# Gated linear attention and a cosine router: rows scattered by expert beside the attention, other block sizes for the experts, and column tiles on TensorE

## The chip, the cores and the metric

The kernel runs on one core of one Trainium2 chip. The metric is the time of one execution on the device in microseconds (us), as the median of several executions; lower is better. A profile of one execution gives its span, from the first to the last instruction.

The engines are TensorE (PE in the rows; PEld is its weight load, a row of its own), VectorE (DVE), ScalarE (ACT), GpSimd (POOL) and SyncE (SP), which issues most of the DMAs. An fp32 matmul stands in the trace as two records, each with a weight load of its own; a transpose on TensorE is one record. "Record" below means this.

## The reference

The first half is a gated linear recurrence with a state of 48 by 48 for each of 4 x 8 heads over 768 tokens. The second half sends each of the 3072 rows of its result (384 columns) to the one of 8 experts whose embedding it resembles most, and runs that expert's two layers on it.

```python
# q, k, v, alpha: (4, 8, 768, 48)
for t in range(S):
    state = alpha[:, :, t, :, None] * state + einsum('bhd,bhe->bhde', k[:, :, t], v[:, :, t])
    y[:, :, t] = einsum('bhd,bhde->bhe', q[:, :, t], state)
x = y.transpose(0, 2, 1, 3).reshape(3072, 384)
logits = normed(x) @ normed(expert_emb).T / tau          # 8 experts
expert_idx = argmax(logits, axis=1)
gate_w = softmax(logits)[arange(N), expert_idx]
for e in range(8):                                       # w1: 384 x 1024, w2: 1024 x 384
    mask = expert_idx == e
    out[mask] = gate_w[mask, None] * (maximum(x[mask] @ w1[e], 0) @ w2[e])
```

Everything is fp32. With the inputs of the reference the experts 0 to 7 get 418, 365, 379, 426, 395, 371, 351 and 367 rows; of the first 16 x 128 tokens expert 0 gets 282.

## The kernel before

**Attention.** The tokens are cut into 24 chunks ("slots") of 128, six for each sequence. A chunk is handled for all eight heads at a time; two heads of 48 columns, padded to 64, fill the 128 partitions, so there are four pairs. A loop over steps `s` (its last lines, after `prepare_experts`) runs four stages of four different chunks in a step: `decays(s)`, `scores(s-1)` and `update(s-1)`, `rows(s-2)`, `logits(s-3)`. `load` fetches alpha, q, k and v two chunks ahead, in pieces of 192 bytes.

- `decays` turns alpha, k and q with TensorE (`turned`, L174: `pa`, `pk`, `pq`, four transposes each). VectorE scans the products of alpha forwards (`a`, L201) and backwards (`r`, L202), each pair of heads by itself: eight scans of 128 columns a chunk. It then makes `kr` (L214) and `qs` (L218).
- `scores` (L267) multiplies `kr` and `qs` head by head: eight matmuls that use 64 of the 128 rows of the array, two of them in different halves. VectorE masks the result (`sm`, L271).
- `update` turns `kr` back (`pkb`, L238), ScalarE copies it (`kb`, L240), four matmuls multiply it with v (`pd`, L243), and the new state is the sum with `decayed` (L231, POOL), on VectorE (L254).
- `rows` makes a chunk of x: four matmuls with the decayed state (L283) and eight with `sm` (L292), all with weights of 128 columns; the rows are copied (L300) and written to DRAM as `x_rows`, in the order of the tokens.
- `logits` turns x (L309) and multiplies it with the embeddings (`pl`, L316). After six chunks `choose` finds the expert and the gate of their tokens.

**Routing**, after the last chunk. `rk` (L348, L351) ranks each token among those of its expert, VectorE makes of it a place in blocks of 128 rows, each expert's last block being filled up, and 24 matmuls (`inv`, L398) invert the sort: which token stands in which row of which block.

**Experts.** There are 31 blocks, as many as 3072 rows can need at most. For each block POOL gathers 128 rows of `x_rows` (`xg`, L459), TensorE turns them (`pxg`, L469), 24 matmuls of 128 moving columns make the first layer (`ph`, L478), ScalarE takes the positive part (L484), eight matmuls of 384 columns make the second layer (`pyo`, L488), VectorE multiplies with the gate (L492), and POOL scatters the rows to the output (L493). SP loads the two weight tensors of a block's expert (L451, L454), where they aren't in the buffer yet.

Nothing in this kernel fixes the order of instructions beyond the order of the code: a scheduler arranges each engine's queue.

Of the kernel before, what the change touches and what calls it, by code (L numbers as in the profile page):

```python
# [15 lines left out]
SP = mybir.EngineType.SP  # L16

# [6 lines left out]
def kernel(  # L24
# [25 lines left out]
    NBLK = (N + E * (P - 1)) // P  # L50
    FAR = 1 << 20  # a row index out of bounds: the row is skipped

    x_rows = nc.dram_tensor("x_rows", (N, DM), FP32, kind="Internal").ap()
# [7 lines left out]
    make_upper_triangular(nc, causal[:, 0], val=1.0, diag=True)  # L61
    earlier = consts.tile([P, P], FP32)  # [j, i] = 1 where j < i
    make_upper_triangular(nc, earlier, val=1.0, diag=False)
    ones = consts.tile([P, P], FP32)
    nc.gpsimd.memset(ones, 1.0)
    zeros = consts.tile([P, P], FP32)
    nc.gpsimd.memset(zeros, 0.0)
    half = consts.tile([P, NP, 2], FP32)  # which head of the pair a partition is of
    nc.gpsimd.memset(half, 0.0)
    nc.gpsimd.memset(half[0:DP, :, 0:1], 1.0)  # L70
    nc.gpsimd.memset(half[DP:P, :, 1:2], 1.0)
    cols_i = consts.tile([P, P], I32)
    nc.gpsimd.iota(cols_i, pattern=[[1, P]], base=0, channel_multiplier=0)
    cols = consts.tile([P, P], FP32)
    nc.vector.tensor_copy(cols, cols_i)
    toks_i = consts.tile([P, NS], I32)
    nc.gpsimd.iota(toks_i, pattern=[[P, NS]], base=1, channel_multiplier=1)
    toks = consts.tile([P, NS], FP32)  # token + 1
    nc.vector.tensor_copy(toks, toks_i)
    first = consts.tile([P, E], FP32)  # E, E-1, ..: the first of equal logits wins  # L80
    nc.vector.tensor_scalar(first, cols[:, 0:E], -1.0, float(E), ALU.mult, ALU.add)

# [1 line left out]
    lg = consts.tile([P, NS, E], FP32)  # L84
    sq = consts.tile([P, NS], FP32)
    gate = consts.tile([P, NS], FP32)
    chosen = consts.tile([P, NS, E], FP32)
    before = consts.tile([P, NS + 1, E], FP32)
    nc.gpsimd.memset(before[:, 0], 0.0)
    rtau = consts.tile([P, 1], FP32)  # L90
    embT = consts.tile([P, KT, E], FP32)
    gidx = consts.tile([P, NBLK], I32)
    sidx = consts.tile([P, NBLK], I32)
    bgate = consts.tile([P, NBLK], FP32)
    eblk = consts.tile([1, NBLK], I32)
    fresh = consts.tile([1, NBLK], I32)

    # ==== gated linear attention, a chunk of P tokens of all heads at a time ====
    with ExitStack() as c1:
        pads = c1.enter_context(tc.tile_pool(name="pads", bufs=1))  # L100
        loads = c1.enter_context(tc.tile_pool(name="loads", bufs=6))
# [3 lines left out]
        ps_mm = c1.enter_context(tc.tile_pool(name="ps_mm", bufs=3, space=PSUM))  # L105

        NBUF = 4
        at_s = [pads.tile([P, H, DP], FP32, name=f"at{i}") for i in range(NBUF)]
        qt_s = [pads.tile([P, H, DP], FP32, name=f"qt{i}") for i in range(NBUF)]
        kt_s = [pads.tile([P, H, DP], FP32, name=f"kt{i}") for i in range(NBUF)]  # L110
        for i in range(NBUF):
            nc.gpsimd.memset(at_s[i][:, :, D:DP], 1.0)
            nc.vector.memset(qt_s[i][:, :, D:DP], 0.0)
            nc.vector.memset(kt_s[i][:, :, D:DP], 0.0)
        NR = 3
        r_s = [pads.tile([P, NP, P], FP32, name=f"r{i}") for i in range(NR)]
        for i in range(NR):
            nc.vector.memset(r_s[i][:, :, P - 1 : P], 1.0)
# [4 lines left out]
        def prepare_experts():  # L123
            emb = work.tile([E, DM], FP32, name="emb", bufs=1)
            nc.scalar.dma_start(out=emb, in_=expert_emb)
            nc.scalar.dma_start(out=rtau, in_=tau.to_broadcast([P, 1]))
            nc.vector.reciprocal(rtau, rtau)
# [405 lines left out]
```

## Time and profile before

| what | us |
|---|---|
| median of 3 runs (the runs: 627.73, 634.01, 628.14) | 628.14 |
| span of the profiled execution | 625.4 |
| TensorE busy in it | 554.2 |
| VectorE busy | 201.9 |
| ScalarE busy | 100.9 |
| GpSimd busy | 93.7 |

The span is the only time that the profile gives of its own execution; the median of the runs lies 2.7 us above it, and what stands around the first and the last instruction is taken to be that. "Busy" is the time in which at least one instruction of the engine ran; matmuls are pipelined, so the time that a group of them takes is read from the start of its first record to the start of the first record of the next group, not from the durations. [...]

### The profile page before, as it was taken

Reading aid. Unit: us, or ns where it says so; the run is one execution under the profiler, and the core shown is the slowest. Engines: PE = TensorE matmul, PEld = TensorE weight load, DVE = VectorE, ACT = ScalarE, POOL = GpSimd, SP = SyncE. Lnnn points to the kernel's source line nnn. Section 1 sums busy time; section 2 is a strip of 40 time slices with the busy share of each in tenths; the row PEclk is TensorE's granted clock in tenths of the full one; section 3 lists DMA queues with packets and bytes.
Section 4 is the critical chain, followed back from the end, with each engine's and each line's share of the span. In section 5 each row is a group of like instructions: output and inputs, shape, how many; then the busy total and the mean of one; then the engine's idle time right before and its main releaser. Section 6 shows DMA issues by size and latency. Waiting matters only on the chain.

```text
span 625.4 us, 9640 instructions
## 1 busy us (share of the span) xinstructions
PE 554.2 (89%) x3804; PEld 463.9 (74%) x3804; DVE 201.9 (32%) x608; ACT 100.9 (16%) x202; POOL 93.7 (15%) x149
## 2 busy tenths in 40 slices
PE   5799989889989965389999999999999999999994
PEld 4688878788878855268778787787877877878773
DVE  6967676757765527101010010100101001010010
ACT  2222422422241240001101011011110100101100
POOL 1110110010011101311011120220211112011010
PEclk9999999988995985579999999999999999999998
DMA  9979886636710000760757658166175775811000
GB/s 152 173 128 150 126 123 124 129 67 124 129 39 14 26 25 2 260 243 26 249 181 244 236 192 275 38 239 219 51 248 195 233 258 166 298 39 38 0 1 0
DMA packets 130508, 85.37 MB, mean 137 GB/s; under 512 B 102199, under 2 KB 121699, under 8 KB 130464
## 3 DMA queue, kind: packets, MB, share of 16 engines
q1 hardware_dynamic: 126336, 73.93, 46.4%
q0 software_dynamic: 3968, 10.82, 4.9%
q8 instruction: 30, 0.49, 0.3%
q14 instruction: 14, 0.11, 0.1%
q10 hardware_dynamic: 160, 0.01, 0.0%
HBM read 122.50 MB, written 10.81 MB: 213 GB/s over the span
## 4 chain that ended last, share of the span: by engine, by line
PE 72%; DVE 13%; issue 8%; ACT 2%; DMA 2%; POOL 1%; POOLq 0%; ACTq 0%
PE ph L478 24%; PE pyo L488 22%; PE py L292 7%; PE py L283 4%; DVE a L201 4%; PE pd L243 3%; DVE r L202 3%; PE pl L316 3%; DMA xg<-x_rows,gidx 2%; PE pa L174 2%; PE inv L398 2%; PE sc L267 2%; DVE kr L214 1%; PE px L309 1%; DVE xgT L471 1%
## 5 line engine op out<-in xcount | busy, mean ns | idle before, releaser
L478 PEld LDWEIGHTS ph<-xgT,w 128*128 128x128 f32 x1488 | 172.1, 194 | 14.3 <-DVE xgT L471 9.8
L478 PE MATMUL ph<-xgT,w 128*128 128x128 f32 x1488 | 174.6, 278 | 6.8 <-DVE xgT L471 6.8
L488 PE MATMUL pyo<-w,hT 128*128 128x384 f32 x496 | 165.1, 486 | 0.0
L488 PEld LDWEIGHTS pyo<-w,hT 128*128 128x128 f32 x496 | 91.9, 190 | 57.5
L492 DVE TENSOR_SCALAR y<-pyo,bgate 128x384 f32<-128x384 f32 x31 | 19.2, 618 | 303.1 <-PE pyo L488 303.1
L484 ACT ACTIVATE hT<-ph 128x512 f32<-128x512 f32 x62 | 37.0, 597 | 345.2 <-PE ph L478 345.2
L493 POOL DMA_INDIRECT out_dram<-y,sidx x31 | 31.1, 1003 | 178.8 <-DVE y L492 175.2
L292 PE MATMUL py<-vt,sm 128*128 128x48 f32 x384 | 56.4, 277 | 0.0
L292 PEld LDWEIGHTS py<-vt,sm 128*128 128x128 f32 x384 | 53.0, 203 | 0.0
L459 POOL DMA_INDIRECT xg<-x_rows,gidx x31 | 32.2, 1037 | 135.4 <-PE pxg L469 115.0
L201 DVE TENSOR_TENSOR_SCAN a<-pa,zeros 128x128 f32<-128x128 f32 x96 | 38.9, 405 | 22.0 <-PE pa L174 22.0
L202 DVE TENSOR_TENSOR_SCAN r<-pa,zeros 128x127 f32<-128x127 f32 x96 | 38.1, 397 | 0.0
L283 PE MATMUL py<-decayed,qs 128*128 128x96 f32 x160 | 35.6, 306 | 0.0
L271 DVE TENSOR_TENSOR sm<-sc,causal 128x512 f32<-128x512 f32 x48 | 31.1, 679 | 1.9 <-PE sc L267 1.9
L267 PE MATMUL sc<-qs,kr 64*128 64x128 f32 x384 | 30.6, 302 | 0.0
L267 PEld LDWEIGHTS sc<-qs,kr 64*128 64x128 f32 x384 | 25.6, 203 | 4.7 <-issue 3.8
L243 PE MATMUL pd<-vt,kb 128*128 128x96 f32 x160 | 23.3, 290 | 4.7 <-ACT kb L240 4.7
L231 POOL TENSOR_TENSOR decayed<-state,ends 128x384 f32<-128x384 f32 x20 | 16.6, 830 | 71.1 <-DVE state L254 56.9
L238 PE MATMUL pkb<-ident,kr 128*128 128x128 f32 x80 | 13.4, 291 | 15.5 <-DVE r L202 15.5
L469 PE MATMUL pxg<-ident,xg 128*128 128x128 f32 x93 | 15.0, 298 | 13.7 <-issue 8.5
L218 DVE SCALAR_TENSOR_TENSOR qs<-pq,rend,a 128x128 f32<-128x128 f32 x96 | 27.0, 341 | 0.0
L243 PEld LDWEIGHTS pd<-vt,kb 128*128 128x128 f32 x160 | 20.0, 196 | 8.9 <-ACT kb L240 8.9
(115 smaller groups left out, 382.4 us busy)
## 6 DMA issues: line engine op xcount, KB each, us to landing
w<-in_moe_w_dram SPq DMA_DIRECT2D x62, 1536.0 KB
at<-in_alpha_dram SPq DMA_DIRECT2D x24, 192.0 KB
qt<-in_q_dram SPq DMA_DIRECT2D x24, 192.0 KB
kt<-in_k_dram SPq DMA_DIRECT2D x24, 192.0 KB
vt<-in_v_dram SPq DMA_DIRECT2D x24, 192.0 KB
x_rows<-x SPq DMA_DIRECT2D x24, 192.0 KB
xg<-x_rows,gidx POOLq DMA_INDIRECT x31, 5.4
out_dram<-y,sidx POOLq DMA_INDIRECT x31, 3.0
```

What stands on the lines that cost most here:

```text
L201: nc.vector.tensor_tensor_scan(a[:, p], pa[:, p], zeros, 1.0, ALU.mult, ALU.add)
L202: nc.vector.tensor_tensor_scan(r[:, p, P - 2 :: -1], pa[:, p, P - 1 : 0 : -1], zeros[:, 0 : P - 1], 1.0, ALU.mult, ALU.add,)
L243: nc.tensor.matmul(pd[:, 2 * p * D : 2 * (p + 1) * D], lhsT=kb[:, p], rhs=vt[:, 2 * p : 2 * p + 2].rearrange("p h d -> p (h d)"), start=Tr ...
L267: nc.tensor.matmul(sc[:, hh, p], lhsT=kr[sl, p], rhs=qs[sl, p], start=True, stop=True)
L271: nc.vector.tensor_tensor(sm[:, hh], sc[:, hh], causal.to_broadcast([P, NP, P]), ALU.mult)
L283: nc.tensor.matmul(py[:, 2 * p * D : 2 * (p + 1) * D], lhsT=qs[:, p], rhs=decayed[:, p].rearrange("p j e -> p (j e)"), start=not opened, s ...
L292: nc.tensor.matmul(py[:, h * D : (h + 1) * D], lhsT=sm[:, hh, p], rhs=vt[:, h], start=not opened, stop=True, skip_group_check=True,)
L459: nc.gpsimd.indirect_dma_start(out=xg, out_offset=None, in_=x_rows, in_offset=bass.IndirectOffsetOnAxis(ap=gidx[:, j : j + 1], axis=0), bo ...
L478: nc.tensor.matmul(ph[:, f], lhsT=w1_t[:, i, (f0 + f) * P : (f0 + f + 1) * P], rhs=xgT[:, i], start=(i == 0), stop=(i == KT - 1),)
L484: nc.scalar.activation(hT[:, f0 : f0 + 4], ph, AF.Relu)
L488: nc.tensor.matmul(py, lhsT=hT[:, f], rhs=w2_t[:, f], start=(f == 0), stop=(f == FT - 1))
L493: ins = nc.gpsimd.indirect_dma_start(out=out, out_offset=bass.IndirectOffsetOnAxis(ap=sidx[:, j : j + 1], axis=0), in_=y, in_offset=None, ...
```

## The change

It rewrites most of the kernel; the mathematics stays.

- **Rows scattered beside the attention.** The chunks are put into ten groups of one to three (`GROUPS`). After a group's rows are there, `choose` and `place` find each token's expert and rank, and POOL scatters the rows, with logits and token number (393 columns), to `xs`, where each expert has a region of 3072 rows (`to_rows`). The routing at the end, the gather and the inversion of the sort go.
- **Two early blocks.** After 16 chunks the first expert with 256 rows leads (`first_expert`). Its first 256 rows are fetched and its weights loaded during the attention; the first layer of these two blocks runs in the last three steps (`first_layer_early`), where chunks run out.
- **Three static blocks an expert.** Each expert then gets 384 rows in one go, the leading one 128: the first layer has 384 moving columns. Where an expert has more rows, a branch that TensorE, ScalarE, VectorE, POOL and SP each take by a value in memory runs a half block of 64 rows (`run_extra`); anything beyond that is in `run_rest`, behind another branch. By the counts above the experts 0, 3 and 4 need one half block each, and `run_rest` isn't entered. The rows of a block lie one behind the other in `xs` and are fetched by plain DMAs (`fetch`); `pads` fills up the last block with blank rows. Gates are worked out from the fetched rows (`gates`).
- **Scans over all pairs.** Row 0 of alpha and a second operand restart the product at each pair's border, so a chunk needs one scan of 511 and one of 512 columns. `qs` moves to POOL, the copy of `pq` and half of the mask to ScalarE and POOL.
- **Column tiles, and y in two banks.** `update`, `mix_states`, `mix_chunk`, `rows` and `half_block` write their results to 64 of the 128 partitions, each matmul with weights of 64 columns; neighbours write to different halves, and y is kept transposed in two PSUM banks (`pyx`). `rows` turns it back and makes the logits in the same matmuls (`sel`).
- **TensorE in written order**: `in_turn` issues each group behind the last TensorE instruction before it.

The core of the diff:

```diff
+    GROUPS = (
+        (0, 3), (3, 6), (6, 9), (9, 12), (12, 14), (14, 16), (16, 19), (19, 21), (21, 23), (23, 24)
+    )
+    S0, EARLY = 16, 2
...
+        def to_rows(rows, x):
+            ins = nc.gpsimd.indirect_dma_start(
+                out=xs,
+                out_offset=bass.IndirectOffsetOnAxis(ap=rows, axis=0),
+                in_=x,
...
-            for p in range(NP):
-                nc.vector.tensor_tensor_scan(a[:, p], pa[:, p], zeros, 1.0, ALU.mult, ALU.add)
-                nc.vector.tensor_tensor_scan(
-                    r[:, p, P - 2 :: -1], pa[:, p, P - 1 : 0 : -1], zeros[:, 0 : P - 1],
-                    1.0, ALU.mult, ALU.add,
-                )
+            nc.vector.tensor_tensor_scan(
+                r[:, L - 2 :: -1], pa[:, L - 1 : 0 : -1], inr[:, L - 2 :: -1],
+                1.0, ALU.mult, ALU.add,
+            )
...
+            by_pool = nc.gpsimd.tensor_tensor(
+                qs.rearrange("p n t -> p (n t)"), d["qc"], a, ALU.mult
+            )
...
+        def update(s):
...
+                    mm(
+                        pd[DP * hh : DP * hh + DP, p],
+                        lhsT=kb[:, h * DP : (h + 1) * DP],
+                        rhs=vt[:, h],
+                        start=True, stop=True,
+                    )
...
+        def mix_states(s):
...
+                            mm(
+                                pyx[hh][to : to + DP, q * P : (q + 1) * P],
+                                lhsT=dec[sl, p], rhs=d["qs"][sl, p],
+                                start=(q == 0), stop=False, skip_group_check=True,
+                            )
...
+        def mix_chunk(s):
...
+                    mm(
+                        pyx[hh][to : to + DP, q * P : (q + 1) * P],
+                        lhsT=vt[:, 2 * p + hh], rhs=sm[hh][:, p],
+                        start=("dec" not in d and q == 0), stop=True, skip_group_check=True,
+                    )
...
+        def rows(s):
...
+                        mm(
+                            px[sl, hh, q], lhsT=yT[hh][:, q, sl], rhs=sel[:, hh, q],
+                            start=True, stop=True, skip_group_check=True,
+                        )
...
+        def first_layer(w1_t, hT, xT, f, n):
+
+            ph = ps_h.tile([P, 512], FP32, name="ph")[:, 0:n]
+            for i in range(KT):
+                nc.tensor.matmul(
+                    ph, lhsT=w1_t[:, i, f * P : (f + 1) * P], rhs=xT[:, i],
+                    start=(i == 0), stop=(i == KT - 1),
+                )
...
+        def half_block(w1_t, w2_t, xT, gate, col):
...
+                        for i in range(2):
+                            c0 = (f0 + f) * P + i * HALF
+                            nc.tensor.matmul(
+                                ph[i * HALF : (i + 1) * HALF, f * HALF : (f + 1) * HALF],
+                                lhsT=w1_t[:, k, c0 : c0 + HALF], rhs=xT[:, k],
+                                start=(k == 0), stop=(k == KT - 1), skip_group_check=True,
+                            )
...
+        def run_extra(i):
...
+            with tc.If(more > 0):
+                half_block(
...
-        for j in range(NBLK):
...
+        for i in range(E):
+            if i + 2 < E:
+                weights(i + 2)
+                to_rows(pads[:, i + 2 : i + 3], blank)
+                fetch(i + 2)
+            run(i)
+            run_extra(i)
+            if i == 3:
+                run_rest(i % NW)
```

How the instructions stand now. TensorE, one chunk in the middle of the attention, before (L174 turns, L267 scores, L238 turns `kr` back, L309 turns x, L243 is the state, L283 and L292 are the rows):

```order
L174 MATMUL pa<-ident,at_123 128x128 x4
L174 MATMUL pk<-ident,kt_131 128x128 x4
L174 MATMUL pq<-ident,qt_127 128x128 x4
L267 MATMUL sc<-qs,kr 128x128 x8
L238 MATMUL pkb<-ident,kr 128x128 x4
L309 MATMUL px<-ident,x 128x128 x3
L243 MATMUL pd<-vt,kb 128x96 x4
L283 MATMUL py<-decayed,qs 128x96
L292 MATMUL py<-vt,sm 128x48 x2
```

The last two rows come three times more, and then `pl` (three matmuls). The same engine and place now (line numbers are those of the changed kernel, where all matmuls of the attention are recorded at L187 and all transposes at L190; `dec` is the decayed state, `ycols` the transposed y):

```order
L187 MATMUL pyx_478<-qs,dec 64x128
L187 MATMUL pyx_479<-qs,dec 64x128
L187 MATMUL pyx_478<-sm_370,vt_128 64x128 x4
L187 MATMUL pyx_479<-sm_371,vt_128 64x128 x4
L187 MATMUL pd<-vt_129,kb 64x64 x8
L187 MATMUL px<-sel,ycols_488 64x104 x4
L187 MATMUL px<-sel,ycols_489 64x104 x4
L190 MATMUL pkb<-ident,kr 128x128 x4
L190 MATMUL pa<-ident,at_115 128x128 x4
L190 MATMUL pk<-ident,kt_123 128x128 x4
L190 MATMUL pq<-ident,qt_119 128x128 x4
```

The first two rows stand there four times in turn, and eight matmuls of the scores follow behind `pq`. The rows of a chunk and its state have become 32 matmuls with results on 64 partitions, and the turn of x and the logits are one group, `px`.

TensorE, from the last chunk to the first expert, before:

```order
L309 MATMUL px<-ident,x 128x128 x3
L316 MATMUL pl<-embT,xT 128x8 x3
L348 MATMUL rk<-before,ones 128x200
L351 MATMUL rk<-chosen,earlier 128x192
L398 MATMUL inv<-put,in_row 128x62 x24
L469 MATMUL pxg<-ident,xg 128x128 x15
L478 MATMUL ph<-xgT,w_0_2664 128x128 x24
L488 MATMUL pyo<-w_0_2666,hT 128x384 x8
```

And now (`phe` is the early first layer; the `pyo` rows before L843 are the second layers of the two early blocks):

```order
L187 MATMUL rk<-before,ones 128x16
L187 MATMUL rk<-chosen,earlier 128x16
L187 MATMUL phe<-exT,w_0_93 128x256 x6
L187 MATMUL rk<-before,ones 128x8
L187 MATMUL rk<-chosen,earlier 128x8
L187 MATMUL rk<-before,ones 128x8
L187 MATMUL phe<-exT,w_0_93 128x256 x6
L854 MATMUL pyo<-w_0_95,ehT 128x384 x10
L796 MATMUL pxg<-ident,xg_90 128x128 x3
L796 MATMUL pxg<-ident,xg_90 128x64 x3
L854 MATMUL pyo<-w_0_95,ehT 128x384 x6
L843 MATMUL ph<-xT_2981,w_0_93 128x128 x6
```

Between the last `rk` and the first `pxg`, which needs rows that are still to be scattered and fetched, there now stand 6 + 10 matmuls of the early blocks.

TensorE, in the middle of the experts, before:

```order
L478 MATMUL ph<-xgT,w_0_2664 128x128 x24
L488 MATMUL pyo<-w_0_2666,hT 128x384 x8
L469 MATMUL pxg<-ident,xg 128x128 x6
L478 MATMUL ph<-xgT,w_1_2665 128x128 x24
L488 MATMUL pyo<-w_1_2667,hT 128x384 x8
```

And now, the end of one expert's turn (L873 and L886 are the half block, which L923 jumps over where it isn't needed):

```order
L843 MATMUL ph<-xT_2982,w_1_94 128x384 x6
L796 MATMUL pxg<-ident,xg_92 128x128 x3
L843 MATMUL ph<-xT_2982,w_1_94 128x384 x6
L796 MATMUL pxg<-ident,xg_92 128x64 x3
L854 MATMUL pyo<-w_1_96,hT 128x384 x24
L919 TENSOR_LOAD extra
L923 COMPARE_AND_BRANCH
L873 MATMUL ph<-xT_2982,w_1_94 64x64 x48
L886 MATMUL pyo<-w_1_96,hT_half 64x384 x8
L923 UNCONDITIONAL_BRANCH x2
```

One expert is one run of 24 + 24 matmuls of 384 columns with the next expert's transposes between them.

## Rows read from the trace of the kernel before

**Rows 1.** Busy time and clock by stage: attention, routing, experts (windows).
```profile
core 0: us, PE busy (x) PEld busy (x) DVE busy (x) ACT busy (x) POOL busy (x), PEclk, DMA share, GB/s
15.00:222.00 207.00, 183.94 (x1593) 167.47 (x1592) 141.85 (x437) 54.80 (x124) 23.90 (x57) 0.94 0.59 103
222.00:270.00 48.00, 21.74 (x114) 19.16 (x115) 18.12 (x69) 5.71 (x12) 9.97 (x14) 0.59 0.35 128
270.00:612.00 342.00, 335.25 (x2048) 267.93 (x2047) 31.72 (x58) 36.42 (x61) 55.72 (x55) 0.99 0.48 163
```

**Rows 2.** Timeline of TensorE, one chunk at full clock (start, length, what).
```profile
100.04 1.13 PE L243 MATMUL pd<-vt,kb 128*128 128x96 f32 x8
101.01 0.39 PE L283 MATMUL py<-decayed,qs 128*128 128x96 f32 x2
...
103.65 0.80 PE L316 MATMUL pl<-embT,xT 128*128 128x8 f32 x6
104.30 0.63 PE L174 MATMUL pa<-ident,at 128*128 128x128 f32 x4
104.77 0.60 PE L174 MATMUL pk<-ident,kt 128*128 128x128 f32 x4
105.21 0.60 PE L174 MATMUL pq<-ident,qt 128*128 128x128 f32 x4
105.74 1.16 PE L267 MATMUL sc<-qs,kr 64*128 64x128 f32 x16
106.83 0.46 PE L283 MATMUL py<-decayed,qs 128*128 128x96 f32 x2
```

**Rows 3.** Two stretches of 2 us around a fall of the clock (windows).
```profile
130.00:132.00 2.00, 0.52 (x10) 0.33 (x6) 2.00 (x10) 0.24 (x1) 0.33 (x2) 1.00 0.85 174
136.00:138.00 2.00, 2.00 (x12) 2.00 (x11) 0.00 (x0) 0.00 (x0) 0.66 (x1) 0.50 0.00 0
```

**Rows 4.** Chain that ended last, in order of time (start, length, what).
```profile
34.66 0.85 PE pl L316 x6
...
143.82 1.72 PE sc L267 x16
...
371.41 5.62 PE ph L478 x48
377.03 5.16 PE pyo L488 x16
382.20 5.36 PE ph L478 x48
387.55 5.18 PE pyo L488 x16
```

**Rows 5.** Groups by line and shape (busy us, mean ns of one; idle before).
```profile
L201 DVE TENSOR_TENSOR_SCAN a<-pa,zeros 128x128 f32<-128x128 f32 x96 | 38.9, 405 | 22.0 <-PE pa L174 22.0
L231 POOL TENSOR_TENSOR decayed<-state,ends 128x384 f32<-128x384 f32 x20 | 16.6, 830 | 71.1 <-DVE state L254 56.9 <-ACT state L252 14.2
L214 DVE TENSOR_TENSOR kr<-pk,r 128x512 f32<-128x512 f32 x24 | 16.5, 689 | 0.5
L240 ACT COPY kb<-pkb 128x512 f32<-128x512 f32 x20 | 11.7, 587 | 73.0 <-PE pkb L238 73.0
```

**Rows 6.** Timeline from the last chunk to the first expert, and the end.
```profile
227.53 0.83 PE L316 MATMUL pl<-embT,xT 128*128 128x8 f32 x6 [0.57 <-ACT xT L313]
...
230.94 0.21 DVE L157 TENSOR_TENSOR chosen<-sel,best 128x48 f32<-128x48 f32 x1
...
242.07 10.50 PE L398 MATMUL inv<-put,in_row 128*128 128x62 f32 x48 [7.51 <-POOL put L393]
...
253.99 1.21 POOL L459 DMA_INDIRECT xg<-x_rows,gidx  x1 [11.97 <-DVE sidx L411]
...
270.40 7.63 PE L478 MATMUL ph<-xgT,w 128*128 128x128 f32 x48
...
617.57 0.62 DVE L492 TENSOR_SCALAR y<-pyo,bgate 128x384 f32<-128x384 f32 x1 [9.90 <-PE pyo L488]
618.47 0.98 POOL L493 DMA_INDIRECT out_dram<-y,sidx  x1 [9.54 <-DVE y L492]
```

**Rows 7.** DMA early in the attention (window), and the scatters of the output.
```profile
15.00:20.00 5.00, 4.33 (x44) 3.80 (x44) 4.26 (x12) 1.07 (x2) 0.83 (x1) 1.00 1.36 170
...
DMA to landing us min/median/max: 2.1/3.0/7.9
```

More of the change, by code (lines that the diff above doesn't have):

```diff
@@ L80 @@
+    part = consts.tile([P, 1], FP32)
+    starts_i = consts.tile([P, NC + 1], I32)
+    starts = consts.tile([P, NC + 1], FP32)
+    blank = consts.tile([P, ROW], FP32)
     first = consts.tile([P, E], FP32)
[L81 to L86, printed above, removed]
+    ebase = consts.tile([P, E], FP32)
     chosen = consts.tile([P, NS, E], FP32)
     before = consts.tile([P, NS + 1, E], FP32)
-    nc.gpsimd.memset(before[:, 0], 0.0)
@@ new lines, with weights @@
+    NW = 3
+    w1_s = [consts.tile([P, KT, F], FP32, name=f"w1_{i}") for i in range(NW - 1)]
+    w2_s = [consts.tile([P, FT, DM], FP32, name=f"w2_{i}") for i in range(NW - 1)]
+    w1_r = w1.rearrange("e (k p) f -> e p k f", p=P)
+    w2_r = w2.rearrange("e (k p) d -> e p k d", p=P)
+    def weights(i):
+        e = nc.values_load(
+            turn_i[0:1, i : i + 1], engines=(SP,), min_val=0, max_val=E - 1,
+            skip_runtime_bounds_check_because="a sum of two experts, less E from E on",
+        )
+        nc.sync.dma_start(
+            out=w1_s[i % NW], in_=w1_r[ds(e, 1)].rearrange("e p k f -> (e p) k f")
+        )
+        nc.sync.dma_start(
+            out=w2_s[i % NW], in_=w2_r[ds(e, 1)].rearrange("e p k d -> (e p) k d")
+        )
@@ new lines, in fetch_early, with mm @@
+    def fetch_early():
+        lead = nc.values_load(
+            turn_i[0:1, 0:1], engines=(SP,), min_val=0, max_val=E - 1,
+            skip_runtime_bounds_check_because="a sum of two experts, less E from E on",
+        )
+        ins = nc.sync.dma_start(
+            out=xg_s[NXG - 1][:, 0:EARLY],
+            in_=xs[ds(lead * N, EARLY * P)].rearrange("(t p) r -> p t r", p=P),
+        )
+        tc.add_to_no_dep_group("xs", ins.ins)
+    last = {}
+    def mm(*args, **kwargs):
+        last["pe"] = nc.tensor.matmul(*args, **kwargs)
@@ L258, in scores @@
+            carried["state"] = state = work.tile([P, NP, DP], FP32, name="state")
+            if c == 0:
+                nc.vector.tensor_copy(state, pd)
+            else:
+                nc.vector.tensor_tensor(state, pd, d["dec"], ALU.add)
         def scores(s):
@@ L325, with warm @@
+        def warm(n):
+            pw = ps_mm.tile([P, P], FP32, tag="mm", name="pw")
+            for _ in range(n):
+                mm(pw, lhsT=ident, rhs=ident, start=True, stop=True)
+        send = []
+        warm(7)
+        fixed_parts()
         load(0)
+        a0 = prepare_loads()
+        prepare_fills()
         load(1)
-        prepare_experts()
         for s in range(NS + 3):
-            if s + 2 < NS:
+            if s + 2 <= NS:
                 load(s + 2)
+            if 0 <= s - 1 < NS:
+                with in_turn():
+                    keys_back(s - 1)
@@ new lines, in second_layer @@
+        def second_layer(w2_t, hT, gate, col, last=False):
+            py = ps_y.tile([P, DM], FP32, name="pyo")
+            y = yp.tile([P, DM], FP32, name="y")
+            for f in range(FT):
+                nc.tensor.matmul(
+                    py, lhsT=hT[:, f], rhs=w2_t[:, f], start=(f == 0), stop=(f == FT - 1),
+                )
+            cut = DM // 2 if last else DM
+            nc.vector.tensor_scalar(y[:, 0:cut], py[:, 0:cut], gate, None, ALU.mult)
+            if last:
+                nc.scalar.mul(y[:, cut:], py[:, cut:], gate)
+            scatter(y, col)
```

924 lines of the change are left out of this document (608 added, 316 removed).

## The prediction

> **What bounds the kernel now.** I read the windows by stage first, then the timeline of TensorE within a chunk, the chain that ended last, the groups by shape, and the hand-off from the last chunk to the first expert.
>
> The windows show three stages [rows 1]. In the attention TensorE is busy 183.94 of 207 us, in the experts 335.25 of 342; in the 48 us of routing it is busy for less than half, at 0.59 of its clock. So two stages are worth what they cost TensorE, and the third is a chain of others. The chunks come every (227.53 - 34.66) / 23 = 8.39 us, from the first `pl` to the last [rows 4, 6].
>
> Inside a chunk the price is the record, not the columns it moves [rows 2]. From start to start, `pd` takes 0.97 us for 8 records of 96 columns (0.121), the 24 records of `py` 2.64 us (0.110, though most move 48), `pl` 0.65 for 6 records of 8 columns (0.108), four transposes 0.47 (0.117). Only `sc`, whose neighbours use different halves of the array, is cheaper: 16 records in 1.09 us, 0.068 each. In the experts the first layer takes 5.36 to 5.62 us for 48 records of 128 columns (0.112), the second 5.16 for 16 of 384 (0.323) [rows 4]; there the columns do count, 0.323 for three times 0.112. [...]
>
> In the hand-off, the last `pl` is at 227.53, the last choice at 230.94, the inversion takes 10.50 us from 242.07, the first gather is issued at 253.99, and the first layer starts at 270.40 [rows 6].
>
> **The attention.** A chunk now has on TensorE 16 transposes x 0.117 = 1.87; the scores as before, 1.09; `mix_states`, 16 records; and `mix_chunk`, `pd` and `px` with 16 records each, their results on 64 partitions, their weights 64 columns wide. No row shows such a record. It is bounded by 0.110, where halves don't overlap at all, and by 0.034, half of `sc`'s price, as the weights are half as wide. The nearest row is `sc`, two tiles at a time; I take 0.060, a little under its 0.068, and 0.050 for `mix_states`, which has four places in the array. That is 48 x 0.060 + 0.80 = 3.68. Changing between tile shapes costs about 0.09: from the first `pq` to the first `sc` it is 0.53 us, against 0.44 for `pk` [rows 2]; five changes make 0.4. In all 7.04. The first chunk of a sequence has no `mix_states`, the last no `pkb` and `pd`: (0.80 + 0.47 + 0.96) x 4/24 = 0.37 less. I add 0.2 for waits in the written order: the bank of `pa` comes free only after the second scan, and every third chunk VectorE's choice stands ahead of it. So 6.87 us a chunk instead of 8.39.
>
> The others stay below. VectorE: a scan of 512 columns is at most four of 0.405 [rows 5], 1.62; two of them, `kr` and a mask at 0.69 each, and the state with some ten small operations, for which I allow 1.3, make 5.9 at most, and its eight scans of before were 3.2 of it. ScalarE: three copies of 512 at 0.587 and three smaller, 3.0. POOL: `qs` and `dec` at 0.830 per 384 columns [rows 5], 1.1 + 0.6, a mask of 512 at the same price per column, 1.1, a scatter of 1.0 [rows 6], and fills, 4.4. DMA: 786 KB of loads and 201 KB of scattered rows at the 170 GB/s of 15 to 20 us [rows 7] are 5.8. If TensorE's records came at 0.034, this 5.8 would be the bound, and nothing under it is to be had.
>
> Start: q of chunk 3 lies behind 2.95 MB at 170 GB/s, 17.3 us and a landing of at least 2.1 [rows 7], so step 3 starts at about 20, and step 24 at 20 + 21 x 6.87 = 164.3. The last steps hold 48 records of the early first layer at 256/384 x 0.323 = 0.215 (10.3), one more `sc` (1.1), the rows of two chunks (5.4), `rk` (1.1) and 6 transposes (0.7): to 182.9.
>
> **The hand-off.** Routing, gather and inversion go; late next is the leading expert's remaining rows. After the last `rk`: three VectorE operations (0.9), three scatters and a blank one, 1.0 each behind each other on POOL, a landing of 3.0, 0.4 that I allow for SP's values and issue, another landing of 3.0 [rows 6, 7]: 11.3. TensorE has meanwhile 12 records of 0.215 and 20 of 0.323, 9.0. So 2.3 us of waiting; with landings of 7.9 it would be 12, with 2.1 nearly none. Queued behind the waiting `pxg` are the second early block and all experts, so a wait here is paid in full. Early second layers 32 x 0.323 = 10.3, 6 transposes 0.7, the wait: to 196.2.
>
> **The experts.** Leading expert: 5.4 + 5.2 and 12 transposes, 1.4: to 208.2. Seven times 96 records of 0.323 are 217.1, with 72 transposes 8.4: to 433.7. That is 24 blocks instead of 31; the first layer's own gain, three of 0.112 for one of 0.323, is nothing worth the name. Three half blocks: 96 records at 0.060 (5.8), 0.7 waiting for ScalarE, 16 records at about 0.17 (2.8): 9.3 each, 28, to 461.6. They save little against a whole block of 10.5. No row shows a branch on TensorE; between nothing (it is taken while matmuls are still queued) and a landing of 3.0 each I take 0.4, as the queue ahead is 24 matmuls, eight times: 3.2. Weights, 3.1 MB per 31 us, and the gates stay beside it. The end stays: from the last y at 617.57 to 625.4 [rows 6], 8. Sum 472.8, against the span of 625.4; with the 2.7 that the median lies above the span, **475 us**.
>
> [...]
>
> **Rivals.**
> - *Each change of shape drains.* A record's length is 0.63 - 3 x 0.117 = 0.28 [rows 2]; five make 1.4 instead of 0.4, and 24 chunks 24 us more: 499. Against it: only 0.09 is seen at `sc`.
> - *The halves don't overlap.* 0.110 instead of 0.060: (24 + 24 + 20) x 16 x 0.05 = 54, `mix_states` 20 x 16 x 0.06 = 19, half blocks 3 x 7.2 = 22: 571. For it: every full-height record costs 0.11; against it: `sc`.
> - *The clock stays low in the attention.* At 0.50 `sc` takes 1.72 [rows 4], 1.58 times 1.09; 6.87 x 0.58 x 24 = 95 more: 570. For it: a fall after 2 us of little work [rows 3]; against it: that wait was for VectorE's eight scans and choice, which shrink.
> - *Slower than before*: records on 64 partitions run one behind the other at their full length. There are 68 x 16 + 20 x 16 + 3 x 112 = 1744; at 0.28 each, 0.22 more, the time is 859. It is slower from 153 / 1744 + 0.060 = 0.148 us a record on. Nothing in the trace is pipelined so badly.
> - *Not what it says*: if a half block were entered for all eight experts, five more of 9.3 make 521; the counts of rows say three.
>
> **How the numbers follow.** Forecast 0.67; changes that drain 0.12; no overlap 0.09; low clock 0.07; eight half blocks 0.01; slower 0.03; within 1% (about what a measurement of this kernel tells from no change) 0.01, for a mixture of the dear ones. The cheap end is 5.8 a chunk, 22 less, and half blocks 10 cheaper: 443. The high end takes in the draining changes, all of the hand-off's 10 and branches' 14: 525. Left out are the two cases at 570 and what is slower, 0.2.
>
> **What would show it.** Right: `pxg` of the leading expert near 190 us, chunks 6.9 apart, `mix_chunk`, `pd` and `px` near 0.06 a record, a run of 24 + 24 matmuls in 31 us, clock at 1.00 from chunk 3 on. Wrong: TensorE waiting in the chunks for VectorE or POOL, records near 0.11, the clock at 0.50 for long, or gaps of some us behind each expert's last `pyo`.

## The result and the profile after

The changed kernel takes 453.01 us (median of 4 runs, 451.56 to 453.83), the kernel before beside it 630.39; the ratio is 0.7182 with a 95% interval of 0.7134 to 0.723. The forecast was 475, the range 443 to 525. The profiled execution has a span of 451.3, and TensorE is busy for 431.3 of it.

The stages of the changed kernel (windows; they answer to [rows 1]; columns as there):

```profile
15.00:162.00 147.00, 141.57 (x2161) 122.39 (x2159) 110.41 (x241) 67.82 (x141) 91.97 (x160) 1.00 0.95 190
162.00:168.30 6.30, 6.30 (x36) 5.71 (x35) 3.66 (x30) 1.63 (x4) 2.96 (x3) 1.00 0.18 64
168.30:443.20 274.90, 271.14 (x1195) 162.37 (x1194) 46.27 (x158) 78.44 (x173) 33.27 (x34) 0.99 0.31 107
```

The stage of routing, 48 us at a clock of 0.59 before, is gone, and TensorE's granted clock (PEclk, as a share of its full speed) is 0.99 to 1.00 in all three. Its timeline shows one chunk (answering to [rows 2]), the hand-off ([rows 6]), one half block and the branch behind it:

```profile
94.71 1.16 PE L187 MATMUL sc<-qs,kr 64*128 64x128 f32 x16
95.80 0.67 PE L187 MATMUL pyx<-qs,dec 64*64 64x128 f32 x16
96.40 1.09 PE L187 MATMUL pyx<-sm,vt 128*64 128x128 f32 x16
97.32 0.64 PE L187 MATMUL pd<-vt,kb 128*64 128x64 f32 x16
97.78 0.89 PE L187 MATMUL px<-sel,ycols 128*64 128x104 f32 x16
98.60 0.66 PE L190 MATMUL pkb<-ident,kr 128*128 128x128 f32 x4
99.09 0.60 PE L190 MATMUL pa<-ident,at 128*128 128x128 f32 x4
99.53 0.61 PE L190 MATMUL pk<-ident,kt 128*128 128x128 f32 x4
99.99 0.66 PE L190 MATMUL pq<-ident,qt 128*128 128x128 f32 x4
100.57 1.16 PE L187 MATMUL sc<-qs,kr 64*128 64x128 f32 x16
...
161.09 0.94 PE L187 MATMUL px<-sel,ycols 128*64 128x104 f32 x16
...
165.45 0.37 PE L187 MATMUL rk<-before,ones 128*128 128x8 f32 x2
165.68 2.84 PE L187 MATMUL phe<-exT,w 128*128 128x256 f32 x12
168.35 6.61 PE L854 MATMUL pyo<-w,ehT 128*128 128x384 f32 x20
174.80 0.82 PE L796 MATMUL pxg<-ident,xg 128*128 128x128 f32 x6
...
296.28 3.02 PE L873 MATMUL ph<-xT,w 128*64 128x64 f32 x96
299.13 3.45 PE L886 MATMUL pyo<-w,hT_half 128*64 128x384 f32 x16
305.74 5.83 PE L843 MATMUL ph<-xT,w 128*128 128x384 f32 x12 [3.16 <-ACTq L936]
311.41 0.49 PE L796 MATMUL pxg<-ident,xg 128*128 128x128 f32 x3
```

From `sc` to `sc` a chunk takes 5.86 us instead of 8.39, and TensorE waits for nothing in it. From start to start, a record with narrow weights costs 0.029 us in `pd` (0.46 / 16), 0.051 in `px`, 0.058 in `mix_chunk`, 0.037 in `mix_states`; changes of the tile shape between groups are contained in these prices. The hand-off shows no wait in front of `pxg`. A half block takes 2.85 + 3.38 = 6.2 us. The one gap is in front of the last but one row: 3.16 us at L936, the branch of `run_rest`, and the 12 records behind it take 5.67 us where the same 12 take 3.97 elsewhere.

The scans, per line ([rows 5]): one of 512 columns takes 1.222 us, as long as three of 128 did (0.405 each).

```profile
L498 DVE TENSOR_TENSOR_SCAN a<-pa,ini 128x512 f32<-128x512 f32 x24 | 29.3, 1222 | 0.8
L502 POOL TENSOR_TENSOR qs<-qc,a 128x512 f32<-128x512 f32 x24 | 30.6, 1276 | 34.0 <-DVE a L498 24.1 <-ACT ycols L607 4.3 <-ACT sm L567 3.9
```

Where the 174.1 us between the two spans come from, with the early blocks' work (12.1 us) counted with the experts:

| stage | before | after | less by |
|---|---|---|---|
| attention, to the end of the last `pl` or `px` | 228.2 | 155.2 | 73.0 |
| routing, to the first matmul of an expert | 42.2 | 1.1 | 41.1 |
| experts, to the last y | 347.2 | 287.1 | 60.1 |
| end | 7.8 | 8.0 | -0.2 |

### The profile page after: what moved, and what is told of

Its sections match the earlier page's. It is cut to its first block, busy times and chain, and to the rows that moved or that the text cites. A ratio compares the mean times of both kernels' runs of the same rounds, so it can differ in the third digit from the quotient of the medians.

```text
span 451.3 us, 9164 instructions
## 1 busy us (share of the span) xinstructions
PE 431.3 (96%) x3474; PEld 301.0 (67%) x3474; DVE 172.5 (38%) x464; ACT 154.7 (34%) x330; POOL 138.3 (31%) x230
## 4 chain that ended last, share of the span: by engine, by line
issue 53%; PE 26%; DVE 7%; POOL 5%; DMA 4%; another core or an unknown queue 2%; ACT 1%; POOLq 1%; DVEq 0%; ACTq 0%
PE pyx L187 6%; PE sc L187 4%; POOL out_dram L781 3%; PE px L187 3%; PE pyo L854 2%; PE pa L190 2%; PE pq L190 2%; PE pk L190 2%; PE pkb L190 2%; DVE r L474 2%; PE phe L187 2%; PE pd L187 1%; DMA xs<-x,dest 1%; DMA out_dram<-y,sx 1%
## 5 line engine op out<-in xcount | busy, mean ns | idle before, releaser
L843 PE MATMUL ph<-xT,w 128*128 128x384 f32 (+1 forms) x384 | 120.8, 466 | 3.8 <-ACTq L936 3.2
L854 PE MATMUL pyo<-w,hT 128*128 128x384 f32 x352 | 115.6, 488 | 0.0
L843 PEld LDWEIGHTS ph<-xT,w 128*128 128x128 f32 x384 | 68.4, 192 | 46.9 <-issue 5.7
L854 PEld LDWEIGHTS pyo<-w,hT 128*128 128x128 f32 x352 | 66.3, 190 | 45.3
L847 ACT ACTIVATE hT<-ph 128x384 f32<-128x384 f32 (+1 forms) x64 | 29.7, 465 | 141.4 <-PE ph L843 141.4
L502 POOL TENSOR_TENSOR qs<-qc,a 128x512 f32<-128x512 f32 x24 | 30.6, 1276 | 34.0 <-DVE a L498 24.1
L474 DVE TENSOR_TENSOR_SCAN r<-pa,inr 128x511 f32<-128x511 f32 x24 | 29.2, 1215 | 5.7 <-PE pa L190 5.5
L498 DVE TENSOR_TENSOR_SCAN a<-pa,ini 128x512 f32<-128x512 f32 x24 | 29.3, 1222 | 0.8
L309 POOL DMA_INDIRECT xs<-x,dest x24 | 24.8, 1032 | 11.2 <-DVE best L332 4.0
L187 PE MATMUL sc<-qs,kr 64*128 64x128 f32 x384 | 28.1, 286 | 0.0
L187 PE MATMUL pyx<-sm,vt 128*64 128x128 f32 x384 | 26.5, 279 | 0.2 <-POOL sm L568 0.2
L187 PEld LDWEIGHTS sc<-qs,kr 64*128 64x128 f32 x384 | 23.5, 189 | 4.2 <-issue 3.4
L187 PEld LDWEIGHTS pyx<-sm,vt 128*64 128x64 f32 x384 | 20.4, 136 | 4.4 <-issue 3.3
L187 PE MATMUL px<-sel,ycols 128*64 128x104 f32 x384 | 21.5, 254 | 0.0
L187 PEld LDWEIGHTS px<-sel,ycols 128*64 128x64 f32 x384 | 17.7, 137 | 1.2 <-issue 0.7
```

The costliest lines, as they stand in the source:

```text
L187: last["pe"] = nc.tensor.matmul(*args, **kwargs)
L309: ins = nc.gpsimd.indirect_dma_start(out=xs, out_offset=bass.IndirectOffsetOnAxis(ap=rows, axis=0), in_=x, in_offset=None, bounds_check=E ...
L474: nc.vector.tensor_tensor_scan(r[:, L - 2 :: -1], pa[:, L - 1 : 0 : -1], inr[:, L - 2 :: -1], 1.0, ALU.mult, ALU.add,)
L498: d["a_scan"] = by_dve = nc.vector.tensor_tensor_scan(a, pa, ini, 0.0, ALU.mult, ALU.add)
L502: by_pool = nc.gpsimd.tensor_tensor(qs.rearrange("p n t -> p (n t)"), d["qc"], a, ALU.mult)
L843: nc.tensor.matmul(ph, lhsT=w1_t[:, i, f * P : (f + 1) * P], rhs=xT[:, i], start=(i == 0), stop=(i == KT - 1),)
```

## Experiments

The question was why the chunks and half blocks came out cheaper than forecast, and what else the 475 had wrong. Spans are compared with the 451.3 of the changed kernel, medians with its 453.0.

**Half blocks without column tiles.**

```diff
-                        for i in range(2):
-                            c0 = (f0 + f) * P + i * HALF
...
-                                ph[i * HALF : (i + 1) * HALF, f * HALF : (f + 1) * HALF],
-                                lhsT=w1_t[:, k, c0 : c0 + HALF], rhs=xT[:, k],
...
+                        c0 = (f0 + f) * P
...
+                            ph[:, f * HALF : (f + 1) * HALF],
+                            lhsT=w1_t[:, k, c0 : c0 + P], rhs=xT[:, k],
```

and the second layer's eight matmuls all write to the lower half, `py[0:HALF]`.

> The half blocks without column tiles: the first layer as 48 records of 64 columns with weights of 128 columns, the second as 16 records of 384 columns. Theory (a record with full-height weights costs 0.112 us however few columns it moves): 48 x 0.112 + 16 x 0.323 = 10.5 instead of 6.23, for three half blocks 13 more: 466. Rival (only columns are paid, 0.029 for 64): 1.4 + 5.2 = 6.6, 1 more: 454.

Measured: 466.09 us (466.01 to 466.22). The timeline of its TensorE, with the next expert's first row as the end:

```profile
191.72 5.47 PE L872 MATMUL ph<-xT,w 128*128 128x64 f32 x48
197.11 5.38 PE L884 MATMUL pyo<-w,hT_half 128*64 128x384 f32 x16
202.42 3.81 PE L843 MATMUL ph<-xT,w 128*128 128x384 f32 x11
```

10.7 us a half block, 0.112 a record of 64 columns (5.39 / 48), as much as the records of 128 columns cost before: at full height 64 columns are no cheaper than 128, and column tiles save 13 us here. The second layer's 16 records, which all write to one half, cost 0.332, against 0.323 at full height, so narrow weights alone made nothing cheaper here.

**The same half for neighbours.**

```diff
-            for p in range(NP):
-                for hh in range(2):
+            for hh in range(2):
+                for p in range(NP):
```

and likewise in `rows` and `half_block` (the half outermost); `mix_chunk` takes the pairs as (0, 2, 1, 3).

> The same column-tile matmuls, with neighbours that write to the same half of the partitions (pd, px, mix_chunk, half blocks; mix_states is left as it is). Theory: the low price (pd 0.029 us a record, px 0.051, mix_chunk 0.058, half block 0.030 and 0.211) is that of two halves at work side by side. Then each doubles: pd +0.46, px +0.82, mix_chunk +0.92 a chunk, 2.2 x 24 = 53, and 6.2 more for each of three half blocks, 19: about 525. Rival 1: a record is paid by the columns that it moves, whatever its neighbour: 453, as it is. Rival 2: alone, a record costs the 0.110 of a full-height one: (16 x 0.110 x 3 - 2.2) x 24 = 74 and (96 x 0.110 + 16 x 0.323 - 6.2) x 3 = 29 more: about 555.

Measured: 469.12 us (467.96 to 469.33), between all that was expected.

```profile
100.36 1.14 PE L187 MATMUL pyx<-sm,vt 128*64 128x128 f32 x16
101.28 0.74 PE L187 MATMUL pd<-vt,kb 128*64 128x64 f32 x13
```

`mix_chunk`, now four records to one half and four to the other, still takes 0.92 for its 16; `pd`, eight and eight, 0.75 (101.28 to 102.03); the half block's first layer, 24 and 24, about 5.0 (199.33 to its last three records at 204.27) instead of 2.85. None doubled. That the halves work side by side survives only if records for the other half start ahead of their turn, as a `px` at 101.81 does here, ahead of two `pd` written before it that start at 101.86, and that was tested.

**Long runs in one half.**

```diff
-            for hh in range(2):
-                for p in range(NP):
+            for p in (0, 2, 1, 3):
+                for hh in range(2):
```

in `mix_chunk`, and `rows` with `lhsT=yT[hh][:, q]` of 128 columns.

> Two parts. mix_chunk writes eight records to one half, then eight to the other (in the changed kernel two and two; in the run same_half four and four, which cost nothing, 0.92 us for the 16), and both copies of y come behind them. rows is written with full-height weights of 128 columns: 8 records of 104 columns instead of 16. Theory: each half of the array works off its own records one behind the other at the price of a full-height one, 0.84 ns a column, 0.108 for 128; the halves run side by side as long as TensorE finds a record for the other half among the next three or four. Then the 16 records of mix_chunk take (16 - 3.5) x 0.108 = 1.35 instead of 0.92; in same_half so did pd (0.75 instead of 0.46) and px. The rows cost 8 x 0.108 = 0.86 instead of 0.82, as full-height records of few columns do. With up to 0.5 more a chunk for the later copies, 24 x (0.47 to 0.97): 464 to 476. Rival: a 128-column record costs 0.058 with narrow weights in whatever order: mix_chunk stays at 0.92, and 454 to 466.

Measured: 464.50 us (462.91 to 465.05). Timeline of its TensorE:

```profile
103.20 1.25 PE L187 MATMUL pyx<-sm,vt 128*64 128x128 f32 x13
104.18 0.27 PE L187 MATMUL pd<-vt,kb 128*64 128x64 f32 x1
104.29 0.27 PE L187 MATMUL pyx<-sm,vt 128*64 128x128 f32 x1
104.29 0.22 PE L187 MATMUL pd<-vt,kb 128*64 128x64 f32 x1
104.40 0.27 PE L187 MATMUL pyx<-sm,vt 128*64 128x128 f32 x1
104.40 0.27 PE L187 MATMUL pd<-vt,kb 128*64 128x64 f32 x1
104.51 0.27 PE L187 MATMUL pyx<-sm,vt 128*64 128x128 f32 x1
104.51 0.73 PE L187 MATMUL pd<-vt,kb 128*64 128x64 f32 x13
105.17 1.14 PE L187 MATMUL px<-sel,ycols 128*128 128x104 f32 x8
106.15 0.60 PE L190 MATMUL pkb<-ident,kr 128*128 128x128 f32 x4
```

The last three records of `mix_chunk`, in the upper half, start every 0.11 us, and beside them `pd` already runs in the lower half, though it is written behind them. `mix_chunk` takes 104.51 + 0.11 - 103.20 = 1.42 us, by the theory (16 - 3) x 0.108 = 1.40. So in these runs the price is that of the full array, 0.84 ns a column (0.108 / 128; in the kernel before 5.18 / 16 / 384 [rows 4]), once for each half, and work for the other half starts up to three records ahead of its turn: two and two or four and four, the 16 take 0.92, eight and eight 1.42. `px` at full height takes 0.98 and the `pkb` behind it 0.43, together 0.10 more than the 0.82 + 0.49 with tiles: there tiles bring next to nothing.

**More changes of the tile shape.** `mix_states` and `mix_chunk` mixed, first two and two (120 more changes), then four and four (40 more).

```diff
+            for q in range(NQ):
+                for j in range(2):
+                    for i in range(2):
+                        state_mm(i, 2 * q + (i + j) % 2)
+                    for i in range(2):
+                        chunk_mm(i, 2 * q + (i + j) % 2)
```

> mix_states and mix_chunk are mixed, two matmuls of the one and two of the other in turn, neighbours still in different halves: six more changes of the tile shape in each of the 20 chunks that have a state, 120 in all, and no other work. Theory (the rows of the changed kernel show hardly more than 0.1 us at a change): between 0 and 120 x 0.09 = 11 more, 453 to 464. Rival, that each change drains the engine for the 0.28 us of a record's length: 34 more, 487.

Measured: 482.74 us (482.56 to 483.68), above the theory's 464 and near the rival's 487. Its timeline:

```profile
96.49 0.44 PE L187 MATMUL pyx<-qs,dec 64*64 64x128 f32 x4
96.86 0.44 PE L187 MATMUL pyx<-sm,vt 128*64 128x128 f32 x4
97.23 0.44 PE L187 MATMUL pyx<-qs,dec 64*64 64x128 f32 x4
...
99.06 0.44 PE L187 MATMUL pyx<-sm,vt 128*64 128x128 f32 x4
99.33 0.64 PE L187 MATMUL pd<-vt,kb 128*64 128x64 f32 x16
```

The eight groups take 2.84 us instead of 1.52. Two records on each of two places are 0.216, and a group takes 0.37, so 0.15 is the change; but the states also lost two of their four places here. The second run keeps those, with four groups of eight records:

> mix_states and mix_chunk in turn by q: four matmuls of the states (all four places of the array, as before), four of the chunk (halves in turn), and once more: two more changes of the tile shape in each of 20 chunks, 40 in all, and nothing else. Theory, from the run with 120 more changes (29.7 us more, of which 20 x 0.44 because the states there used two places at a time instead of four): 0.15 to 0.17 a change, 6.4 more, 459.5. Rival 1: all of the 29.7 was changes, 0.25 each: 10 more, 463. Rival 2: all of it was the lost places: 453.

Measured: 458.71 us (456.45 to 459.10), span 457.0: 5.7 for 40 changes, 0.14 each.

```profile
98.09 0.45 PE L187 MATMUL pyx<-qs,dec 64*64 64x128 f32 x8
98.47 0.66 PE L187 MATMUL pyx<-sm,vt 128*64 128x128 f32 x8
99.06 0.45 PE L187 MATMUL pyx<-qs,dec 64*64 64x128 f32 x8
99.44 0.66 PE L187 MATMUL pyx<-sm,vt 128*64 128x128 f32 x8
99.92 0.64 PE L187 MATMUL pd<-vt,kb 128*64 128x64 f32 x16
```

The rows agree: the 32 records take 1.83 us instead of 1.52, 0.155 for each of two changes. That is more than a row of the unchanged order lets see, and half of the rival's 0.28.

**No written order.**

```diff
-        return tc.issue_after(last["pe"].ins) if last else ExitStack()
+        return ExitStack()
```

> TensorE's written order is taken out (in_turn does nothing), the scheduler arranges the matmuls of the attention as it did in the kernel before. Theory: the records' sum, 5.87 us a chunk, stays the bound, and the order only keeps TensorE from waiting; with the share of idle time of the attention before, 23 of 207 us, the 140 us of attention become some 155: 468. Rival: the order is worth nothing, as the scheduler finds the same: 453. Other rival: the early blocks and chunks get into each other's way and the hand-off is exposed: 11 more on top, near 480.

Measured: 454.25 us (453.46 to 454.79), chunks of 5.87 us in the same sequence. The first theory falls: the scheduler finds the order in which the code stands, and `in_turn` is worth nothing that can be measured.

**The branch of `run_rest`.**

```diff
-            if i == 3:
+            if i == E - 1:
```

> run_rest stands behind the last expert instead of behind the fourth. In the changed kernel TensorE waits 3.16 us at its branch, and the 12 records behind it take 5.67 us instead of 3.97, with the clock at 0.54. Theory: the wait is the jump over run_rest's code, and the clock falls because TensorE idles; at the end both lie beside the last multiplication, copy and scatter: 4.9 less, 448. Rival 1: the jump is paid at the end too, as the program ends behind it: 3.2 back, 451. Rival 2: the wait belongs to the place (weights or rows of the fifth expert are late), not to the jump: 453, with the same gap at 302 us.

Measured: 452.37 us (451.96 to 452.57). The gap at 302 us is gone and the last scatter is issued at 439.51 instead of 444.53, but the span ends at 450.5 instead of 451.3, 11.0 us behind that issue instead of 6.8: the jump is paid there, as the first rival had it.

The trace of the changed kernel shows which jump TensorE waits for. TensorE's own branch at L936 lasts from 300.5 to 304.0 us, the first two of them beside matmuls that are still at work (the last ends at 302.6). But the row names ScalarE's queue: ScalarE comes to the same branch only at 303.2, behind its copy of the half block, and goes on at 305.7, when TensorE does. So the 3.16 us end with ScalarE's jump; TensorE's own ended 1.7 us before. Other runs show the same, as `no_order`, where TensorE waits 3.4 us, ScalarE goes on at 306.2 and TensorE at 306.24.

So the code jumped over was made smaller, in one kernel with the scores on four places:

```diff
-                for i in range(E):
+                with tc.For_i(0, E) as i:
...
-                    mm(
-                        sc[hh][:, p], lhsT=kr[sl, p], rhs=qs[sl, p], start=True, stop=True
...
+                    for to in (0, HALF):
+                        mm(
+                            sc[hh][to : to + HALF, p], lhsT=kr[sl, p, to : to + HALF],
+                            rhs=qs[sl, p], start=True, stop=True, skip_group_check=True,
```

> Two parts, at different places. run_rest's eight written-out experts become one loop over them, so that the code jumped over is an eighth; and the scores are written by 16 matmuls with weights of 64 columns, on the four places of the array that mix_states uses behind them, so that one change of the tile shape a chunk goes. Theory: the wait of 3.16 us at 302 us is the size of the jump, and goes down to the 0.2 of the other branches, with the 1.7 us of low clock behind it: 4.7 less; a change of shape is 0.14 (5.7 us over 40, the run with two more changes a chunk), the scores keep their 1.09 less that: 24 x 0.14 = 3.4 less. Together 445. Rival 1: a jump costs its 3 us whatever its size: 449.6, the gap stays at 302 us. Rival 2: the scores' 32 narrower records cost more than the 16, at 0.054 one behind the other 1.7 us: 15 more, 463 with the jump gone.

Measured: 445.16 us (445.15 to 445.55), ratio 0.7116 (0.7086 to 0.7146); all four runs lie below the lowest of the changed kernel, 451.56; the intervals of the two ratios overlap only from 0.7134 to 0.7146. Its timeline:

```profile
91.76 1.10 PE L187 MATMUL sc<-qs,kr 64*64 64x128 f32 x32
92.68 0.62 PE L187 MATMUL pyx<-qs,dec 64*64 64x128 f32 x16
93.23 1.09 PE L187 MATMUL pyx<-sm,vt 128*64 128x128 f32 x16
...
97.41 1.10 PE L187 MATMUL sc<-qs,kr 64*64 64x128 f32 x32
...
146.06 1.10 PE L187 MATMUL sc<-qs,kr 64*64 64x128 f32 x32
...
299.69 4.11 PE L845 MATMUL ph<-xT,w 128*128 128x384 f32 x12 [0.45 <-PEq L938]
```

A chunk takes 5.65, 0.21 less where 0.14 was expected; the last `sc` starts at 146.06 instead of 149.50, 3.4 us earlier. That this is the expected 3.4 is in part luck: 23 chunks at 0.21 would be 4.8, and why a chunk gained more and the rest did not arrive stays open. The wait behind `run_rest` is 0.45 instead of 3.16, and with the low clock behind it 4.4 us go: TensorE's own branch lasts 0.42 us instead of 3.45, ScalarE goes on 0.5 us after its branch instead of 2.5, and TensorE, at 299.69, doesn't wait for it. Together 7.8, the difference of the spans, 451.3 and 443.5.

**The cover of the hand-off.** The turn of the leading expert's rows is put ahead of the early second layers. In a first run, `pxg_first`, the scheduler left TensorE's order as it was, so its 452.65 us tells nothing; the second orders it.

```diff
+            if t == 0:
+                prepare(0, 0)
...
+            with in_turn():
+                second_layer(
```

> The turn of the leading expert's first block is now really ahead of all 32 records of the early second layers (in the run pxg_first the scheduler had left it between them). Theory: the rows land close to the 174.8 us at which the changed kernel turns them: a wait of 6 at 168.4, 459. Rival: they land with a distance, at 171 to 172: a wait of 3, 456. Other rival: they are there: 453.

Measured: 460.77 us (one run), and on the timeline:

```profile
173.75 0.87 PE L796 MATMUL pxg<-ident,xg 128*128 128x128 f32 x3 [5.43 <-DMA xg<-xs]
```

The rows are there at 173.75, 1.05 us before the changed kernel uses them. The cover of 6.45 us is needed almost whole; without it the wait, and the 16 records behind it, which take 7.1 us where 16 of 384 columns take 5.2 at full clock (granted from 173.75 to 182: 0.73), make up most of the 7.8 by which the span is longer.

**Less work for TensorE in a chunk.**

```diff
-            dec = d.get("dec")
+            d.pop("dec", None)
+            dec = None
```

> mix_states is left out: a chunk's y lacks what the state carries over from earlier chunks (decay_state is still computed). Theory: TensorE's records are the bound of a chunk, and it loses the 0.60 us of 16 records: 20 x 0.60 = 12 less, 441. Rival: the loads bind (DMA busy for 0.99 of the engines' time at 188 GB/s in the attention): a chunk stays at 5.8 or more, 20 x 0.07 = 1 less, 452, and TensorE waits for qt, kt or at.

Measured: 457.77 us (454.42 to 460.63), slower than with the work. Where nothing waits, a chunk does take 5.27 us (`sc` at 92.37 and 97.64), with 182 GB/s moved in that stretch. Later the clock falls to 0.69 behind two waits for POOL of 0.95 and 0.79 us, and the loads stop, as its windows show (columns as in [rows 1]):

```profile
116.00:120.00 4.00, 4.00 (x41) 3.55 (x41) 3.83 (x10) 1.21 (x3) 0.40 (x2) 0.69 0.61 112
124.00:128.00 4.00, 4.00 (x72) 3.73 (x73) 3.13 (x7) 2.42 (x6) 1.78 (x3) 1.00 0.00 0
```

and on the timeline of TensorE:

```profile
148.23 1.09 PE L190 MATMUL pa<-ident,at 128*128 128x128 f32 x4 [8.84 <-DMA at<-in_alpha_dram]
```

No byte moves from 124 to 128 us: on SP's queue the scheduler had put the last chunk's loads behind the fetch of the early rows, which waits for a scatter, and behind 3.1 MB of weights. With the order of the changed kernel:

```diff
-                        fetch_early()
-                        weights(0)
+                        load(s + 3)
+                        load_akq(s + 4)
+                        with tc.issue_after(last["load"].ins):
+                            fetch_early()
+                            weights(0)
```

> mix_states is left out again (a chunk's y lacks what the state carries over), but the loads of the last chunk are issued ahead of the early rows and the leading expert's weights, as they are in the changed kernel; without mix_states alone the scheduler had put them behind, where TensorE waited 8.8 us for alpha. Theory: TensorE's records bound the chunks, 5.27 instead of 5.87: 441. Rival: with DMA at 0.99 in the attention the loads bind, and TensorE waits for at, kt or qt elsewhere: 448 to 453.

Measured: 451.74 us (448.40 to 455.98). Neither theory, though the number lies in the rival's range: TensorE waits no longer for a load, but 5.8 us in all for VectorE's and POOL's part of the choice in front of `rk` (2.6 in the changed kernel), and 2.5 us for POOL's mask near the end. Its executions spread, and the profiled one (span 454.2) is the longest of them; but the run before, `no_states`, waits 6.1 us in front of `rk` in the same way. Of the 12 us that TensorE's records lose here, 1.3 arrive in the median. It isn't so for every gain: in `compact_sc` 3.4 us of 4.8 arrived. What would bound a chunk here if the choice were cheaper stays open.

## Why the prediction was right, and what it had wrong

The mechanism held: TensorE's records set the chunk, nothing else got in front, the routing went under the attention, and the experts are 24 blocks and three halves. In the order of the prediction's terms:

- *Records with narrow weights, "I take 0.060", and 0.050 for `mix_states`.* The size was off, and this is the step that failed. The runs show two halves that each pay 0.84 ns a column: 64 columns 0.029, 104 0.051, 128 0.058, with the changes of shape between the groups in them. So `mix_chunk`, `pd` and `px` take 2.20 us instead of 2.88, `mix_states` 0.60 instead of 0.80, and a chunk 5.86 where 7.04 stood. The price of `sc` was the wrong neighbour: its 0.068 fits 0.054, what 128 columns on two places cost, and the changes around it. Steps 3 to 24 come every (148.72 - 20.02) / 21 = 6.13 us instead of 6.87 (148.72 is the start of the early rows' turn); step 3 started at 20.02, where 20 was forecast, and step 24 at 148.7 instead of 164.3: 15.6 us of the miss. The shorter chunk alone would have made 24.8 (21 x 1.18); 9.2 were given back by `rk`, 3.8, which the sum had only at the end, by waits of 5.0 in all where 0.2 x 21 = 4.2 stood, by the first and last chunks of a sequence, which save 4.7 instead of 7.8, and by some 1.5 of other idle time.
- *Five changes of shape, 0.4.* There are four a chunk at 0.14, 0.56, and they lie within the prices of the groups above. The row from which 0.09 was read shows only part of a change. The first rival's 0.28, a record's length, was the author's estimate from [rows 2]: the runs with added changes show half of it, 0.14 to 0.155 each, and no row shows what that time goes to.
- *DMA's 5.8 as the bound.* Wrong as a floor: it came from 170 GB/s, and in `no_states` chunks of 5.27 us ran at 182 without a wait for loads. VectorE (busy for 110.41 of 147 us), POOL (91.97) and ScalarE (67.82) stayed below, as forecast.
- *Last steps, 18.6.* 19.6 (148.72 to 168.35).
- *Hand-off, a wait of 2.3.* None. TensorE's cover was as forecast (9.1 us from the last `rk` at 165.45 to 174.80, with 0.2 for that `rk`, instead of 9.0), but the chain takes 8.3, not 11.3, as the run without cover shows: from issue to the next step the blank scatter and the fetch took 2.6 us each (168.49 to 171.14 to 173.75), and only one scatter of rows and one blank one stood on it. Early second layers and the turn took 11.2 (168.35 to 179.53) instead of 13.3.
- *Leading expert 12.0, seven experts 225.5, branches 3.2.* 12.1, and 232.9 for the two others together (443.2 - 191.64, less three half blocks) instead of 228.7. A branch that isn't entered shows 0.4 to 0.5 us (15.89 to 16.01 from the start of a second layer's 48 records to the next group, where 48 x 0.323 are 15.5), near the 0.4; but `run_rest` was priced as nothing beyond that and cost 3.16, up to the end of ScalarE's jump, and 1.70 of low clock. No run shows the 14 us for branches that the high end of the range holds; in their place the runs show those 0.4 to 0.5 and the one long jump, whose wait shrank from 3.16 to 0.45 with the code.
- *Half blocks, 9.3 each.* 6.2, three of them 9.3 us less in all: the same step as the first, 2.85 for the first layer's 5.8 (0.030 for the 0.060). The second layer with its wait for ScalarE was right: 3.38 (0.211 a record) where 2.8 + 0.7 stood, and at 299.78 its weight load waits 0.51 for ScalarE.
- *End 8, and 2.7 around the span.* 8.0 and 1.7.

The differences, -15.6 + 1.0 - 2.1 + 0.1 + 4.2 - 9.3 - 1.0, are -22.7, against the 475.5 of the unrounded sum: 452.8. None of the rivals came: the halves overlap, the clock stood at 0.99 and more in every stage, and the half blocks were entered three times. That the time came near the cheap end of the range is in part luck: the 443 took 5.8 us a chunk from the loads, and it was TensorE's own records that came down to 5.86.

## What to carry to other kernels

With column tiles count the columns that each half has to move, at the full array's price per column (0.84 ns here), and write the order so that the halves alternate in short runs (two and two or four and four cost 0.92 us here, eight and eight 1.42); at 64 columns two records side by side cost 0.059 us where one of full height costs 0.112, and at 104 columns tiles brought 0.10 us of 1.41. Count the changes of shape too (0.14 to 0.155 us each here), and put groups of one shape side by side. A rare path kept in the program cost its jump here though it wasn't entered, 3.16 us with eight experts' code and 0.45 with one's, so keep its code short, and look at which engine comes to the branch last; and cover that looks generous (6.45 us here) can be needed but for one.

## What the runs showed that was not expected

- Matmuls started before ones that are written ahead of them and write to the other half: in `long_half` a `pd` at 104.18, ahead of `mix_chunk` records that start at 104.29 to 104.51.
- A jump over code that isn't run cost 3.16 us of TensorE for eight experts' code, 0.45 for one's, and the 3.16 end with ScalarE's jump, not with TensorE's. In the run `half_full` ScalarE and TensorE jump beside TensorE's last matmuls (ScalarE from 306.8 to 309.3, TensorE from 307.3 to 311.2); there the wait is 0.45, and another of 2.51 comes later, at the end of VectorE's jump (312.1 to 318.5).
- After those 3.16 us of idle time the granted clock was 0.54 for the next 3.2 us (window 305.8 to 309), which cost another 1.7.
- Taking work from TensorE made the kernel slower (`no_states`, 457.77 us against 453.01), as the scheduler then put the last chunk's loads behind others on SP's queue.
